# Twelve of sixteen token tiles loaded with columns as rows and normalized there by VectorE

## The chip, the cores and the metric

One Trainium2 chip, one core. The metric is the device time of one execution in microseconds. Engine names as the profile has them: PE is TensorE's matmul (PEld its weight load), DVE is VectorE, ACT is ScalarE, POOL is GpSimd, SP is SyncE, which issues most DMAs. A name with q (SPq, PEq) is the instruction queue of an engine.

## The reference, cut to what matters

```python
x = A_x                                   # 1 x 2048 x 576, float32
xn = layernorm(x)                         # per token: (x - mean) / sqrt(var + 1e-5)
qkv = xn @ wqkv                           # 576 x 1728; 32 heads of 18
phi = lambda t: where(t > 0, t + 1, exp(t)) + 1e-6
kv = einsum("bhsd,bhse->bhde", phi(k), v); z = sum over s of phi(k)
o = (phi(q) @ kv) / (phi(q) @ z + 1e-6)
s = o @ wo
g = silu((gelu(xn @ w_gate) * (xn @ w_up)) @ w_down)   # 576 -> 4608 -> 576
out = x + s * g
```

Every product contracts over the columns of `xn`, so the matmuls want `xn` with its 576 columns on the partitions and the tokens along the free dimension. In memory `x` has one token per row.

## The kernel before, in words

**Tiles.** The 2048 tokens are 16 tiles of 128 (P = 128); four tiles are a block of 512 (TT = 4, TBN = 512), so there are four blocks, `tb` 0 to 3. The 576 columns are two halves of 288 (`j` = 0, 1), each laid out as three chunks of 128 rows, the last 32 rows (KR) repeated to fill the third chunk. A float32 product is made from words: a rounded high word and a low word of each operand, so an operand tile `xo` has five slots (three high chunks, two low ones; the low word of the third chunk stands within it), in tiles named `xo_B`. `xf` holds the same half block in full float32; differences of `xf` tiles (`SUMS`: T1, T3, T2, T4) are operands for a later stage in which the gate and up products are made with fewer multiplications.

**One tile's way.** `load_x` brings a tile with tokens on the partitions. `spread` takes mean and variance on DVE (`bn_stats`, `bn_aggr`) and starts the root on ACT (Ln, Exp); `scales` ends it on DVE; `center` subtracts the mean and multiplies by the scale, one DVE operation of 768 columns with a mean and a scale per partition. `turn` makes six PE transposes (two halves of three chunks) into two PSUM tiles `xt`. `place` copies them on ACT into the high word of `xo` and subtracts on DVE for the low words (a `tensor_sub` of 256 columns on 128 partitions and one of 128 columns on 32, per half). `save` copies the PSUM tiles on ACT into `xf`.

**The stage of the tiles.** `kv_tile(t)` is one round. `x_mm(t, c)`, c = 0 to 2, multiplies tile t by the weights of k and v and of the last columns of q, 14 matmuls each into one PSUM bank. Between them stand `turn(t + 1)`, `place(t + 1)` and `save(t + 1)`; `k_post` (min on DVE into `e_k`, max on DVE into `pk`, Exp on ACT, add on POOL), `v_post` (ACT copies), `kv_mm(t - 1)`, which adds `pk` times `va` into two PSUM banks kept for the whole stage (`kv_a`, `kv_b`), and `q_parts` and `q_post` for the q columns (`w_q`; an add twice on POOL). The q columns of a tile are turned by PE too (`q_turn`), behind the six transposes of `turn`, into a free part of the same PSUM tiles, and copied by `q_keep` into `ph4`. `x_next` is `spread`, `scales` and `center` for the tile two ahead. Tiles 4 to 7 also prepare q's weights (`prep_q`: one ACT copy, three POOL subtractions). Between tiles 7 and 8 stand eight q products (`q_store`), after tile 15 eight more (`q_hold`). `form` builds T1 to T4 of the first two blocks and `keep` stores them in device memory, with SP's DMA queue; `difference` makes the sums.

**Order.** All engines' orders are written out by hand: every operation goes through `pin`, which keeps its engine's program order, and each engine takes its instructions in that order. Waits between engines come from the tiles that the operations share. Tiles of a pool take turns in their buffers: PSUM has six banks of the common kind (`bank`), `b0` to `b15` and `m0` to `m2` are single buffers (`big`, `mid`) that hold one tile after another, so a load into a buffer waits for the last reader of what was in it. The x tiles stand in b14 and b15 by pairs; `xf` of the first two blocks in m0, m1, m2 and b13, of the others in m0, m2, b13 and m1.

**After the tiles.** `den`, `scale`, `halve` and `s_mm` end the attention (up to about 290 us), then 36 gate and up products (`matrix`) and the down product (`down_all`) take the rest. The change touches none of these, but for the place of one helper tile.

The line numbers of the profile: L170 is the transposes of `turn`, L420 those of `q_turn`, L93 all other matmuls of this stage, L87 ACT's operations, L90 DVE's, L96 POOL's, L99 all DMAs.

## Time and profile before

| | |
|---|---|
| time, median of 3 runs (lowest to highest) | 1498.84 us (1497.77 to 1499.46) |
| the profiled execution's own time | 1497.99 us |
| its span, first to last instruction | 1496.3 us |
| PE, DVE, ACT, POOL busy | 1487.2, 1061.4, 561.6, 540.3 us |
| granted TensorE clock, mean over the span | 1.000 |
| transposes of x on PE (L170) | 96, from 8.0 us to 172.5 us |
| transposes of q on PE (L420), beside those of the last two tiles | 14, from 32.4 us to 172.6 us |

A row of the timeline has the start and the length in us, engine, line, operation, the tiles written and read, and how many in a row; in brackets the idle time of the engine before it and what ended it. A row of the groups has count, busy time, mean of one in ns, and idle time in front of them. A row of the waits has who waited for whom, the sum in us, how often, and the longest. Ends of matmuls are modelled, so the distance between two starts is what a PE operation costs.

### The profile page before, as it was taken

The numbers are of one execution on the slowest core, as the hardware profiler recorded it, in microseconds if no ns is written. First come the engines' busy times: TensorE is split into PE (matmuls) and PEld (weight loads), VectorE is DVE, ScalarE is ACT, GpSimd is POOL, SyncE is SP. The second block draws the span as 40 slices with busy tenths as digits, with TensorE's granted clock in tenths as the row PEclk, the third lists the DMA queues.
The fourth block names the chain that finished last, engine by engine and source line by source line (L and its number), as shares of the span: only waits on it lengthen the run. The fifth ranks groups of instructions, "written<-read, shape, count | busy, mean of one in ns | idle before, by whom it ended". The sixth has DMA issues, their size and how long they took to land.

```text
span 1496.3 us, 22479 instructions
## 1 busy us (share of the span) xinstructions
PE 1487.2 (99%) x8399; PEld 1333.1 (89%) x8399; DVE 1061.4 (71%) x1602; ACT 561.6 (38%) x1047; POOL 540.3 (36%) x521
## 2 busy tenths in 40 slices
PE   9999999999999999999999999999999999999998
PEld 8989989988888888888888888888899999999998
DVE  7576476377787877788877788787785466555765
ACT  5435345333222232232232332222445454445443
POOL 5442430145655544655544565554410020000120
PEclk9999999999999999999999999999999999999999
DMA  5423105543443333443423444433697766686873
GB/s 206 147 101 154 58 6 197 193 175 144 172 172 136 144 109 130 173 173 136 160 106 135 154 173 151 157 118 124 216 334 250 233 211 228 227 285 225 298 245 120
DMA packets 112215, 257.15 MB, mean 172 GB/s; under 512 B 10138, under 2 KB 38682, under 8 KB 110058
## 3 DMA queue, kind: packets, MB, share of 16 engines
q1 hardware_dynamic: 110330, 246.41, 46.0%
q0 software_dynamic: 1632, 8.91, 1.6%
q8 instruction: 66, 1.08, 0.3%
q10 hardware_dynamic: 144, 0.39, 0.1%
q14 instruction: 43, 0.35, 0.1%
HBM read 157.73 MB, written 97.91 MB: 171 GB/s over the span
## 4 chain that ended last, share of the span: by engine, by line
PE 97%; DVE 2%; issue 0%; ACT 0%; DMA 0%; POOL 0%; ACTq 0%; DVEq 0%; POOLq 0%
PE bd L971 27%; PE al L765 15%; PE de L765 15%; PE ga L765 15%; PE be L765 8%; PE kv L93 7%; PE s L93 4%; PE q L93 3%; PE kv_a L93 1%; PE xt L170 1%; PE d L93 0%; PE kw L93 0%; PE b L93 0%; DMA x<-in_xe_dram 0%; DVE wkv L90 0%
## 5 line engine op out<-in xcount | busy, mean ns | idle before, releaser
L971 PE MATMUL bd<-t,s 128*128 128x288 f32 x3024 | 401.2, 295 | 0.0
L971 PEld LDWEIGHTS bd<-t,s 128*128 128x128 f32 x3024 | 400.9, 188 | 0.3 <-DVE u L90 0.2
L90 DVE TENSOR_TENSOR s<-sr,s 128x512 fp32r<-128x512 f32 x252 | 176.1, 738 | 119.8 <-ACT s L87 116.0
L87 ACT ACTIVATE s<-sr 128x512 fp32r<-128x512 f32 x252 | 149.0, 626 | 188.9 <-PE bd L971 130.5
L96 POOL TENSOR_TENSOR hs<-h,h 128x512 f32<-128x512 f32 x68 | 94.7, 1402 | 202.5 <-DVE h L90 199.8
L87 ACT ACTIVATE h<-h 128x512 f32<-128x512 f32 x108 | 67.0, 633 | 244.7 <-POOL sm L96 124.1
L96 POOL TENSOR_TENSOR sx<-sx 128x288 f32<-128x288 f32 x24 | 27.9, 1181 | 322.9 <-DVE sx L90 321.8
L93 PE MATMUL kv<-wkv,xo_B 128*128 128x416 f32 (+1 forms) x672 | 130.8, 349 | 0.0
L93 PEld LDWEIGHTS kv<-wkv,xo_B 128*128 128x128 f32 x672 | 121.1, 188 | 1.2 <-POOL wkv L96 0.2
L90 DVE TENSOR_TENSOR wa<-raw,wa 128x256 fp32r<-128x256 f32 x72 | 81.1, 1127 | 51.1 <-ACT wa L87 50.0
L96 POOL TENSOR_TENSOR sm<-raw 128x384 f32<-128x384 f32 x72 | 76.0, 1055 | 109.2 <-DMA raw<-in_wgu_dram 83.5
L90 DVE TENSOR_TENSOR h<-h,u 128x512 f32<-128x512 f32 x108 | 95.7, 886 | 3.7
L87 ACT ACTIVATE wa<-sm 128x1152 fp32r<-128x1152 f32 x36 | 41.8, 1161 | 135.3 <-PE de L765 135.3
L96 POOL TENSOR_TENSOR td<-td 128x288 f32<-128x288 f32 x72 | 70.9, 985 | 51.2 <-DMA td<-in_wd_dram 47.0
L90 DVE TENSOR_TENSOR wa<-sm,wa 128x768 fp32r<-128x768 f32 x72 | 62.9, 873 | 36.9 <-ACT wa L87 36.0
L90 DVE TENSOR_TENSOR wb<-raw,wb 128x256 fp32r<-128x256 f32 (+1 forms) x108 | 73.0, 676 | 7.3 <-ACT wb L87 5.8
L90 DVE TENSOR_TENSOR wb<-sm,wb 128x256 fp32r<-128x256 f32 x72 | 60.9, 845 | 20.6 <-ACT wb L87 20.0
L87 ACT ACTIVATE u<-al 128x512 f32<-128x512 f32 x72 | 40.8, 592 | 88.4 <-PE al L765 88.4
L765 PE MATMUL al<-xo_B,wa 128*128 128x512 f32 x252 | 63.0, 389 | 0.0
L765 PE MATMUL al<-xr_B,wa 128*128 128x512 f32 x252 | 63.0, 389 | 0.0
L765 PE MATMUL be<-xo_T,wa 128*128 128x512 f32 x252 | 63.0, 389 | 0.0
L765 PE MATMUL be<-xr_T,wa 128*128 128x512 f32 x252 | 63.0, 389 | 0.0
(168 smaller groups left out, 2766.5 us busy)
## 6 DMA issues: line engine op xcount, KB each, us to landing
sr<-hs SPq DMA_DIRECT2D x252, 256.0 KB
hs<-h SPq DMA_DIRECT2D x68, 512.0 KB
raw<-in_wgu_dram SPq DMA_DIRECT2D x36, 768.0 KB
hs<-hs SPq DMA_DIRECT2D x102, 256.0 KB
td<-in_wd_dram SPq DMA_DIRECT2D x18, 576.0 KB
td<-td SPq DMA_DIRECT2D x18, 576.0 KB
tr<-td SPq DMA_DIRECT2D x16, 576.0 KB
tr<-in_wd_dram SPq DMA_DIRECT2D x12, 576.0 KB
```

Source lines behind the costliest of these rows:

```text
L87: pin(nc.scalar.activation(*args, **kw))
L90: pin(getattr(nc.vector, op)(*args, **kw))
L93: pin(nc.tensor.matmul(*args, **kw))
L96: pin(getattr(nc.gpsimd, op)(*args, **kw))
L170: pin(nc.tensor.transpose(xts[n][j][:, k, :], xs[:, j, k * P : (k + 1) * P], ident))
L765: nc.tensor.matmul(o, w[0:rows, wi, :], xop[0:rows, xi, :], start=(start and n == 0), stop=(n == len(PASSES) - 1), skip_group_check=True,)
L971: nc.tensor.matmul(banks[j][:, 0:HALF], hw[n, s][:, a, t * P : (t + 1) * P], w[:, c, g % 4], start=(new and g == 0 and m == 0), stop=(g == ...
```

## The change

Tiles 4 to 15 are also given to the kernel as `xt`, the raw x of blocks 1 to 3 with columns as rows, in the layout of `xf`; `load_turned` brings half a block by one DMA (128 x 1536 elements) straight into `xf`. Two tiles at a time, `spread` and `scales` work as before from rows of `x` (576 columns a token, without the repeated ones); then the means and scales of the 256 tokens (512 numbers) go by one DMA into device memory and come back by another onto all 128 partitions, behind the x tiles in their buffer (`mr`). `norm` subtracts and multiplies with them in `xf`: per half block part of two tiles one `tensor_sub` and one `tensor_mul` of 3 x 2 x 128 columns. `place` of these tiles reads `xf` instead of PSUM. `center`, `turn` and `save` are left for tiles 0 to 3 alone: 24 transposes of x instead of 96, each other operation of the product unchanged.

With that move: `q_turn` takes two tiles at once into a bank of its own behind `x_mm(t, 1)` of even tiles, and copies 256 columns; the min in `k_post` goes from DVE to ACT (as Relu of the negative); `place(t + 1)` stands ahead of `x_mm(t, 0)`; `form` also starts the load of a later half block into the buffer it has just read; the differences of the last two blocks stand behind tiles 13 and 15; `load_x(1)` goes from ACT's queue to SP's, ahead of the first weights; `w_q` and a helper tile (`one`) have other buffers.

```diff
@@ -118,18 +119,36 @@
     def load_x(n, k, eng=None):
 
         if n % 2 == 0:
-            xstat[n // 2] = big(14 + n // 2 % 2, [P, 2, 2, 3 * P], F32, f"x_{n}")
-        dma(
-            out=xstat[n // 2][:, n % 2 : n % 2 + k],
-            in_=xe[n * P : (n + k) * P].rearrange("(t p) j d -> p t j d", p=P), eng=eng,
-        )
+            xstat[n // 2] = big(14 + n // 2 % 2, [P, 2 * D + 2 * P2], F32, f"x_{n}")
+        if n < TT:
+            o = x_of(n)[:, None] if k == 1 else xstat[n // 2][:, 0 : 12 * P].rearrange(
+                "p (t j d) -> p t j d", t=2, j=2)
+            dma(out=o, in_=xe[n * P : (n + k) * P].rearrange("(t p) j d -> p t j d", p=P), eng=eng)
+        else:
+            dma(
+                out=xstat[n // 2][:, 0 : 2 * D].rearrange("p (t d) -> p t d", t=2),
+                in_=x[n * P : (n + 2) * P].rearrange("(t p) d -> p t d", p=P),
+            )
+
+    def x_of(n):
+
+        w = 6 * P if n < TT else D
+        return xstat[n // 2][:, n % 2 * w : (n % 2 + 1) * w].rearrange("p (j d) -> p j d", j=2)
+
+    def load_turned(tb, j):
+
+        s, b = divmod(tb, 2)
+        nm = BS[b][j]
+        at_ = XM[s][nm]
+        xf[s][nm] = (mid if at_ < 3 else big)(at_, [P, 3, TBN], F32, f"xf_{s}_{nm}")
+        dma(out=xf[s][nm], in_=xt_d[j, :, :, (tb - 1) * TBN : tb * TBN])
 
     def spread(n0, n):
 
         bn = sb.tile([P, TT, 12], F32, tag="bn", bufs=2, name=f"bn_{n0}")
         mv = sb.tile([P, 2 * TT, 2], F32, tag="mv", bufs=4, name=f"mv_{n0}")
         for t in range(n):
-            xs = xstat[(n0 + t) // 2][:, (n0 + t) % 2]
+            xs = x_of(n0 + t)
             for j in range(2):
                 vec("bn_stats", out=bn[:, t, 6 * j : 6 * j + 6], in_=xs[:, j, 0:HALF])
             vec("bn_aggr", out=mv[:, t, :], in_=bn[:, t, :])
...
@@ -142,6 +161,7 @@
     def scales(n0):
 
         n, mv, st = mom.pop(n0)
+        far = n0 >= TT
...
@@ -150,28 +170,42 @@
         else:
             vec("scalar_tensor_tensor", c, r, -0.5, r, op0=ALU.mult, op1=ALU.mult)
             vec("tensor_mul", c, c, v)
-            vec("scalar_tensor_tensor", c, c, 1.5, r, op0=ALU.add, op1=ALU.mult)
+            o = mv[:, 0:n, 1] if far else c
+            vec("scalar_tensor_tensor", o, c, 1.5, r, op0=ALU.add, op1=ALU.mult)
+        if far:
+
+            d = dr.tile([2, 2, P], F32, name=f"mr_{n0}")
+            dma(out=d.rearrange("t q p -> p (t q)"), in_=mv[:, 0:2, :].rearrange("p t q -> p (t q)"))
+            mr = xstat[n0 // 2][:, 2 * D :]
+            dma(out=mr, in_=d.rearrange("t q p -> (t q p)").partition_broadcast(P))
+            return
         for t in range(n):
             scale_of[n0 + t] = mv[:, t, 0:1], c[:, t : t + 1]
 
...
-    def turn(n, new=bank, q=True):
-
-        xs = xstat[n // 2][:, n % 2]
+    def norm(n, js=(0, 1)):
+
+        tb, t = divmod(n, TT)
+        s, b = divmod(tb, 2)
+        mr = xstat[n // 2][:, 2 * D :].rearrange("p (t q c) -> p t q c", t=2, q=2)
+        for j in js:
+            f = xf[s][BS[b][j]][:, :, t * P : t * P + P2].rearrange("p k (t c) -> p k t c", t=2)
+            for q, op in enumerate(("tensor_sub", "tensor_mul")):
+                vec(op, f, f, mr[:, None, :, q, :].to_broadcast([P, 3, 2, P]))
+
+    def turn(n, new=bank):
+
+        xs = x_of(n)
         tiles = [new(f"xt_{n}_{j}") for j in range(2)]
         xts[n] = [t[:, 0 : 3 * P].rearrange("p (k t) -> p k t", k=3) for t in tiles]
         for j in range(2):
             for k in range(3):
                 pin(nc.tensor.transpose(xts[n][j][:, k, :], xs[:, j, k * P : (k + 1) * P], ident))
...
@@ -182,14 +216,13 @@
             nm = BS[b][j]
             if t == 0 and 0 in words:
                 xo[s][nm] = big(2 * b + j, [P, 5, TBN], F32R, f"xo_{s}_{nm}")
-            o, v = xo[s][nm], xts[n][j]
+            o, v = xo[s][nm], xts[n][j] if n < TT else xf[s][nm][:, :, c]
...
@@ -370,11 +403,11 @@
         o, e, src = pks[t], es[t], pkv[t, c]
         cs = slice(0, TW) if c == 0 else slice(TW, D)
         src = src[:, 0 : cs.stop - cs.start]
-        vec("tensor_scalar", e[:, cs], src, 0.0, None, op0=ALU.min)
+        act(e[:, cs], src, AF.Relu, scale=-1.0)
         vec("tensor_scalar", o[:, cs], src, 0.0, EPS, op0=ALU.max, op1=ALU.add)
         if c == 1:
             es.pop(t)
-            act(e, e, AF.Exp)
+            act(e, e, AF.Exp, scale=-1.0)
             pool("tensor_add", o, o, e)
...
-    def q_turn(ts, banks):
-
-        for t, (b, i) in zip(ts, banks):
-            o = b[:, i * P : (i + 1) * P]
-            pin(nc.tensor.transpose(o, pqt.pop(t)[:, 0:2], ident))
-            pqx[t] = o
-
-    def q_keep():
-        for t in sorted(pqx):
-            tb, i = divmod(t, TT)
-            if i == 0:
-                ph4[tb] = gl_tile([P, TBN], f"ph4_{tb}")
...
+    def q_turn(t):
+
+        tb, i = divmod(t, TT)
+        b = bank(f"qx_{t}")
+        for n in range(2):
+            pin(nc.tensor.transpose(b[:, n * P : (n + 1) * P], pqt.pop(t + n)[:, 0:2], ident))
+        if i == 0:
+            ph4[tb] = gl_tile([P, TBN], f"ph4_{tb}")
+            if tb < 2:
+                ph_d[tb] = dr.tile([P, NHG, TBN], F32, name=f"phd_{tb}")
+        act(ph4[tb][:, i * P : (i + 2) * P], b[:, 0:P2], AF.Copy)
+        if i == 2 and tb < 2:
+            dma(out=ph_d[tb][:, 4, :], in_=ph4[tb])
...
-    def kv_tile(t, mid_=(), end=(), after=()):
-
-        ahead = t % (2 * TT) != 2 * TT - 1
+    def kv_tile(t, early=(), end=(), after=()):
+
+        if t % (2 * TT) != 2 * TT - 1 and t > TT - 1:
+            place(t + 1)
         x_mm(t, 0)
-        if ahead:
-            turn(t + 1)
         k_post(t, 0)
+        run(list(early))
         x_mm(t, 1)
-        if ahead:
+        if t % 2 == 0 and t % (2 * TT):
+            q_turn(t - 2)
+        if t == TT - 1:
             place(t + 1)
-            save(t + 1)
-        run(list(mid_))
         k_post(t, 1)
...
@@ -597,7 +627,7 @@
         buf = big(15, [P, n + TBN], F32R, "aux")
         at["sel"] = sel = buf[:, 0:n].rearrange("p (g j) -> p g j", g=NHG)
         at["rd"] = rd = buf[:, n : n + TBN]
-        at["one"] = one = tmp([H, NHG, P], "self")
+        one = at["one"]
...
@@ -1089,8 +1119,8 @@
 
     turn_idle(22)
     load_x(0, 1)
+    load_x(1, 1)
     load_kv(0, 0)
-    load_x(1, 1, nc.scalar)
     load_kv(0, 1)
...
@@ -1134,6 +1164,8 @@
     x_mm(0, 0, of((1, LO), (1, MIX)))
     x_mm(1, 0, of((1, LO), (1, MIX)))
     load_x(4, 2)
+    for j in range(2):
+        load_turned(1, j)
...
     def x_next(n):
 
-        if n % 2 == 0:
-            spread(n, 2)
-            scales(n)
-        center(n)
-
+        spread(n, 2)
+        scales(n)
+
+    def form(nm, tb, j):
+
+        o = build(0, nm, 12)
+        load_turned(tb, j)
+        keep(0, nm, o)
 
     x_mm(2, 0)
-    turn(3, q=False)
+    turn(3)
     kv_mm(0)
-    q_turn((0,), [(xtb.pop(3)[0], 3)])
     k_post(2, 0)
+    x_next(4)
     x_mm(2, 1)
+    q_turn(0)
     place(3)
     save(3)
     load_x(6, 2)
@@ -1187,25 +1223,33 @@
     v_post(2, 1)
     x_mm(2, 2)
     kv_mm(1)
-    x_next(4)
     v_post(2, 2)
     q_parts(2)
     q_post(2)
...
     for n in range(3, 2 * TT):
-        ends = []
-        if n < 2 * TT - 2:
-            ends.append(lambda n=n: x_next(n + 2))
+        early, ends, after = [], [], []
+        if n == 3:
+            early.append(lambda: norm(4))
+        if n == 3:
+            after.append(lambda: x_next(6))
+        if n == 4:
+            after.append(lambda: norm(6))
         if n >= TT:
             j, c = divmod(n - TT, 2)
             prep_q(c, j)
             if n == TT + 1:
                 load_q(1)
-        if n == 2 * TT - 1:
-            ends += [lambda i=i: difference(0, i) for i in range(3)]
-        kv_tile(n, end=ends)
-        if n in (4, 6):
-            load_x(n + 4, 2)
+        if n == 5:
+            after.append(lambda: x_next(8))
+        if n == 6:
+            after += [lambda i=i: difference(0, i) for i in range(2)]
+        if n == 7:
+            ends.append(lambda: difference(0, 2))
+            after.append(lambda: form("T1", 2, 0))
+        kv_tile(n, early, ends, after)
+        if n in (4, 5):
+            load_x(2 * n, 2)
         if n == TT:
...
     behind = {
         0: [lambda: kv_mm(N0 - 1), lambda: difference(0, 3)],
-        1: [lambda: spread(N0, 2), lambda: scales(N0)],
-        2: [lambda: center(N0), lambda: form("T1")],
-        3: [lambda: spread(N0 + 2, 2), lambda: scales(N0 + 2)],
-        4: [lambda: turn(N0), lambda: place(N0)],
-        5: [lambda: center(N0 + 1), lambda: form("T3")],
-        6: [lambda: save(N0)],
+        1: [lambda: q_turn(N0 - 2)],
+        2: [lambda: form("T3", 2, 1), lambda: norm(N0, (0,))],
+        3: [],
+        4: [lambda: norm(N0, (1,)), lambda: load_x(N0 + 4, 2)],
+        5: [lambda: place(N0)],
+        6: [lambda: x_next(N0 + 2)],
         7: [],
     }
     for i in range(8):
         q_store(*divmod(i, 4))
         run(behind[i])
...
     for n in range(N0, 2 * N0):
-        ends = []
-        if n < 2 * N0 - 2:
-            ends.append(lambda n=n: center(n + 2) if n == N0 else x_next(n + 2))
-        after = [lambda n=n: form("T2" if n == N0 else "T4")] if n in (N0, N0 + 2) else []
+        early, ends, after = [], [], []
+        if n % 2 == 0 and n < 2 * N0 - 2:
+            after.append(lambda n=n: norm(n + 2))
+        if n in (N0, N0 + 1):
+            form_ = ("T2", 3, 0) if n == N0 else ("T4", 3, 1)
+            after.append(lambda f=form_: form(*f))
+        if n in (N0 + 1, N0 + 3):
+            after.insert(0, lambda n=n: x_next(n + 3))
+        if n == N0:
+            after.insert(1, lambda: load_x(N0 + 6, 2))
         if n == 2 * N0 - 3:
             ends.append(load_wo)
+            after.append(lambda: difference(1, 0))
         if n == 2 * N0 - 2:
             after.append(make_sel)
         if n == 2 * N0 - 1:
-            after.append(copy_sel)
-            ends += [lambda i=i: difference(1, i) for i in range(3)]
-        kv_tile(n, end=ends, after=after)
-        if n in (N0, N0 + 2):
-            load_x(n + 4, 2)
-    def last_turn():
-        b = bank("q_last")
-        q_turn(sorted(pqt), [(b, 0), (b, 1)])
-        q_keep()
+            after += [copy_sel, lambda: difference(1, 1), lambda: difference(1, 2)]
+        kv_tile(n, early, ends, after)
 
     q_hold(2, 7, [
-        [lambda: kv_mm(2 * N0 - 1), kv_done, last_turn, lambda: difference(1, 3)],
+        [lambda: kv_mm(2 * N0 - 1), kv_done, lambda: q_turn(2 * N0 - 2), lambda: difference(1, 3)],
         [lambda: kv_wo(4)],
...
@@ -1341,6 +1382,8 @@
     xs = A_x.reshape(S, D)
     xh = xs.reshape(S, 2, HALF)
     xe = np.concatenate([xh] + 3 * [xh[:, :, 2 * P :]], axis=2)
+    xt = xe[TBN:].reshape(S - TBN, 2, 3, P).transpose(1, 3, 2, 0)
+    xe = xe[:TBN]
```

More of the change, by code (lines that the diff above doesn't have):

```diff
@@ L170, in turn @@
                 pin(nc.tensor.transpose(xts[n][j][:, k, :], xs[:, j, k * P : (k + 1) * P], ident))
-        if q:
-            q_turn([t for t in sorted(pqt) if t < n - 1], [(t, 3) for t in tiles])
-        else:
-            xtb[n] = tiles
     def place(n, js=(0, 1), words=(0, 1)):
@@ L348, in block_kernel @@
     left = {}
-    pkv, pks, vas, es, pqt, pqx, ph4, ph, ph_d = ({} for _ in range(9))
+    pkv, pks, vas, es, pqt, ph4, ph, ph_d = ({} for _ in range(8))
     def x_mm(t, c, passes=None, new=bank):
@@ L401, in q_parts @@
     def q_parts(t):
-        w = tmp([P, 4, Q4], f"w_q{t}")
-        src, o, e = pkv[t, 2][:, CW[2] - Q4 : CW[2]], w[:, 2], w[:, 3]
+        w = sb.tile([P, 3, Q4], F32, tag="wq", bufs=3, name=f"w_q{t}")
+        src, o, e = pkv[t, 2][:, CW[2] - Q4 : CW[2]], w[:, 0], w[:, 2]
         vec("tensor_scalar", e, src, 0.0, None, op0=ALU.min)
@@ L411, in q_post @@
         w = pqt[t]
-        act(w[:, 3], w[:, 3], AF.Exp)
-        for i in range(2):
-            pool("tensor_add", w[:, i], w[:, 2], w[:, 3])
-    def q_turn(ts, banks):
-        for t, (b, i) in zip(ts, banks):
-            o = b[:, i * P : (i + 1) * P]
-            pin(nc.tensor.transpose(o, pqt.pop(t)[:, 0:2], ident))
-            pqx[t] = o
-    def q_keep():
-        for t in sorted(pqx):
-            tb, i = divmod(t, TT)
-            if i == 0:
-                ph4[tb] = gl_tile([P, TBN], f"ph4_{tb}")
-                if tb < 2:
-                    ph_d[tb] = dr.tile([P, NHG, TBN], F32, name=f"phd_{tb}")
-            act(ph4[tb][:, i * P : (i + 1) * P], pqx.pop(t), AF.Copy)
-            if i == TT - 1 and tb < 2:
-                dma(out=ph_d[tb][:, 4, :], in_=ph4[tb])
+        act(w[:, 2], w[:, 2], AF.Exp)
+        for i in (1, 0):
+            pool("tensor_add", w[:, i], w[:, 0], w[:, 2])
+    def q_turn(t):
[10 more added lines that the diff above has]
+            dma(out=ph_d[tb][:, 4, :], in_=ph4[tb])
     def run(todo, n=None):
```

17 lines of the change are left out of this document (8 added, 9 removed).

## The prediction

> **What bounds the kernel now.** I read the page first: how busy each engine is, and the chain of work that ended last.
>
> ```profile
> PE 1487.2 (99%) x8399; PEld 1333.1 (89%) x8399; DVE 1061.4 (71%) x1602; ACT 561.6 (38%) x1047; POOL 540.3 (36%) x521
> PE 97%; DVE 2%; issue 0%; ACT 0%; DMA 0%; POOL 0%; ACTq 0%; DVEq 0%; POOLq 0%
> ```
>
> PE is busy for 1487.2 of 1496.3 us and 97% of the chain. So what PE need not do comes off the end, if the engines that feed it still deliver in time. The stage to read is the one from 20 to 190 us, where the 16 token tiles pass. This is PE's timeline there, around tiles 5, 6 and 7 (columns: start, length, operation, count, and in brackets what ended idle time).
>
> ```profile
> 61.19 5.34 PE L93 MATMUL kv<-wkv,xo_B 128*128 128x416 f32 x28
> ...
> 70.05 0.82 PE L170 MATMUL xt<-ident,x 128*128 128x128 f32 x6
> 70.71 0.27 PE L420 MATMUL xt<-ident,w_q 128*128 128x128 f32 x1
> 70.74 5.34 PE L93 MATMUL kv<-wkv,xo_B 128*128 128x416 f32 x28
> ...
> 76.89 7.96 PE L93 MATMUL kv<-wkv,xo_B 128*128 128x416 f32 x42
> 84.69 1.05 PE L93 MATMUL kv_a<-pk,va 128*127 128x126 f32 x8
> ...
> 85.67 1.41 PE L93 MATMUL q<-xo_B,wq 128*128 128x512 f32 x5
> ```
>
> No row has a bracket: PE runs without a gap. From 61.19 to 70.74 is one tile with its six turns of x and one turn of q, 9.55 us. Tile 7 turns nothing and takes 76.89 to 85.67, 8.78 us. Where PE does wait in this part is in the view of waits up to 230 us:
>
> ```profile
> PE xt L170 <- DVE x L90: 1.6, 2, 1.3
> PE xt L420 <- POOL w_q L96: 0.4, 1, 0.4
> PE q_last L420 <- POOL w_q L96: 0.3, 1, 0.3
> ```
>
> **What goes from PE.** Seven turns make 9.55 - 8.78 = 0.77 us, so six make 0.66; the same comes out of the starts, 70.05 to 70.71. The change takes away `turn` of tiles 4 to 15: 12 x 0.66 = 7.9 us, none of it beside other PE work. The 16 turns of q stay, now in pairs behind `x_mm(t, 1)`: no change counted.
>
> **Waits that go.** Of the two waits of 1.6 us for DVE's x, the longest (1.3) is for the very first tile; the other 0.3 is `turn(2)`. In the new order the min of `e_k` has left DVE, so `center(2)` no longer queues behind it. The turn of q tile 0 (0.4) now stands one `x_mm` later. The last turn (0.3) waited because three differences stood ahead of `q_parts(15)` on DVE; now they stand behind it. Together 1.0 us. What is late next: nothing within 2 us, since each of these turns then has its operand before PE reaches it.
>
> **The start.** `load_x(1)` moves from ACT's queue to SP's, ahead of the first weights. The first tile no longer shares the DMA engines with it and lands earlier, the weights behind it land when they did, as the bytes ahead of them are the same. The gain lies between 0 and the 1.3 us above; I take 0, because PE's next matmuls need those weights, not x.
>
> **What DVE gets.** These are DVE's, POOL's and ACT's groups of the stage 113 to 187.5 us (the second eight tiles), one of POOL's from 38 to 77, and the busy time of the stage (PE, PEld, DVE, ACT, POOL).
>
> ```profile
> L90 DVE TENSOR_SCALAR x<-x,mv,st 128x768 f32<-128x768 f32 x6 | 4.1, 680 | 0.2
> L90 DVE TENSOR_SCALAR e_k<-kv 128x416 f32<-128x416 f32 x8 | 4.7, 593 | 12.6 <-PE kv L93 9.8 <-POOL w_q L96 2.7
> L90 DVE TENSOR_SCALAR e_k<-kv 128x160 f32<-128x160 f32 x8 | 2.6, 324 | 4.6 <-PE kv L93 4.5
> L90 DVE TENSOR_TENSOR xo_T<-xf_B,xo_T 128x1024 fp32r<-128x1024 f32 x3 | 4.0, 1348 | 3.8 <-ACT xo_T L87 3.8
> L90 DVE TENSOR_TENSOR xo_T<-xf_B,xo_T 32x512 fp32r<-32x512 f32 x3 | 2.0, 681 | 0.0
> L90 DVE TENSOR_TENSOR xo_B<-xt,xo_B 128x256 fp32r<-128x256 f32 x14 | 6.0, 425 | 0.9
> L90 DVE TENSOR_TENSOR xo_B<-xt,xo_B 32x128 fp32r<-32x128 f32 x14 | 4.0, 283 | 0.4
> L90 DVE BATCH_NORM_STATS2 bn<-x 128x6 f32<-128x288 f32 x8 | 3.2, 438 | 0.1
> L90 DVE BATCH_NORM_AGGREGATE mv<-bn 128x2 f32<-128x12 f32 x4 | 0.8, 209 | 0.1
> L90 DVE SCALAR_TENSOR_TENSOR st<-st 128x2 f32<-128x2 f32 x4 | 0.7, 162 | 0.9 <-ACT st L87 0.8
> L96 POOL TENSOR_TENSOR pk<-pk,e_k 128x576 f32<-128x576 f32 x8 | 12.4, 1546 | 40.9 <-ACT e_k L87 40.9
> L96 POOL TENSOR_TENSOR w_q<-w_q 128x64 f32<-128x64 f32 x14 | 4.2, 321 | 6.7 <-ACT w_q L87 6.7
> L96 POOL TENSOR_TENSOR wq<-rq,wq 128x256 fp32r<-128x256 f32 x3 | 2.2, 735 | 1.0 <-ACT wq L87 0.7
> L87 ACT ACTIVATE xo_B<-xt 128x384 fp32r<-128x384 f32 x14 | 6.1, 490 | 14.2 <-PE xt L420 14.2
> L87 ACT ACTIVATE st<-mv,eps_t 128x2 f32<-128x2 f32 x2 | 0.6, 296 | 2.3 <-DVE mv L90 2.3
> L87 ACT ACTIVATE st<-st 128x2 f32<-128x2 f32 x2 | 0.4, 203 | 0.1
> 113.00:187.50 74.50, 74.50 (x457) 73.81 (x456) 43.34 (x110) 33.52 (x100) 24.65 (x44) 1.00 0.29 107
> ```
>
> DVE is busy 43.34 of 74.5 us, so 5.55 us in a tile of 9.55. Of that `center` (0.68) and the two mins of `e_k` (0.59 + 0.32) go. What comes is `norm`: four tensor-tensors of 768 columns for two tiles. No row has 768; 512 take 0.68, 1024 take 1.35, so about 1.01 each, 2.0 us a tile. DVE then has 5.55 - 0.68 - 0.91 + 2.0 = 6.0 us in a tile of PE that is now about 8.78 + 0.11 = 8.9: two thirds. ACT loses two saves as long as its 0.49 us copy and takes the mins, 416 and 160 columns, for about 0.53 + 0.30: no more than before, 33.52 of 74.5 us. So on the averages neither becomes the bound, and DVE's new work is covered by PE's. What decides is whether one tile's chain is late.
>
> **The new wait.** Mean and scale go out by one DMA in 4-byte pieces and come back by another that waits for it; `norm` stands first in line on DVE and waits for the second. Queued behind it on DVE are `place` of the next tile and the `pk` of `k_post`, and PE waits for `place`. On SP, the load of the next pair, `load_q` and the stores of `ph4` queue behind the reading back; none is needed within a tile. Three rows bound a round trip: the first load, and the last stores at the end of the span.
>
> ```profile
> core 0 of [0], span 1496.3 us
> 0.81 0.39 SPq L99 DMA_DIRECT2D x<-in_xe_dram  x1
> 4.81 0.82 DVE L90 BATCH_NORM_STATS2 bn<-x 128x6 f32<-128x288 f32 x2 [4.81 <-DMA x<-in_xe_dram]
> 1493.11 0.89 SPq L99 DMA_DIRECT2D out_dram<-sx  x2
> ```
>
> From issue to use is 4.0 us for the first load, among others; the last store is issued by 1494.0 and the span ends 2.3 us later. Two in a row: 4.6 to 8.0 us. Mine are small, but in 512 pieces: I take 6, nearer the short one.
>
> How long may it take? The statistics of a pair cost 4 x 0.44 + 2 x 0.21 on DVE, 0.30 + 0.20 on ACT and four small DVE operations of 0.16: about 3.3 us. For pairs 6, 10, 12 and 14 they run behind tile n and `norm` behind tile n + 1, a PE tile later: 8.9 - 3.3 = 5.6 us before DVE stands still. After that `norm` (4.0) and `place` (2 x (0.43 + 0.28) = 1.4) must be done in the 8.9 us of the next tile: 3.5 us to spare. PE is late only from 9.1 us on. Pair 4 has its statistics behind `x_mm(2, 0)` and its `norm` behind `x_mm(3, 0)`: a tile, a `turn` and one `kv_mm` (84.69 to 85.67, 1.0 us) apart, 8.9 + 0.66 + 1.0 - 3.3 = 7.3; behind it only two thirds of a tile are left, some 6 us for the 5.4: about 7.9. Pair 8 has the whole q stage. At 6 us all fit with 2 us or more, at 8.0 only just.
>
> That room is shared with POOL. Here are DVE and POOL when tile 7 ends, where DVE runs tensor-tensors with both inputs in SBUF:
>
> ```profile
> 83.02 6.43 DVE L90 TENSOR_TENSOR xf_B<-xf_B,xf_B 128x1536 f32<-128x1536 f32 x3
> 90.83 1.75 DVE L90 TENSOR_TENSOR xf_B<-xf_B,xf_B 128x1536 f32<-128x1536 f32 x1
> ...
> 83.67 2.37 POOL L96 TENSOR_TENSOR pk<-pk,e_k 128x576 f32<-128x576 f32 x1 [3.33 <-ACT e_k L87]
> ```
>
> One costs 1.75; three cost 6.43 instead of 5.25, and POOL's add takes 2.37 where its mean is 1.55: each waited for the other. `norm`, and `place` of tiles 4 to 15, which now reads `xf` in SBUF where it read PSUM (0.43 us with no such spread), become operations of this kind. POOL brings 1.55 + 2 x 0.32 = 2.2 us into a tile, and 3 x 0.735 more in tiles 4 to 7 where it prepares q's weights. At most that much is lost in a tile: 2.2 of a room of some 2.5, 4.4 in tiles 4 and 6. Tiles 8 and 9 also have a `form` (1.35 + 0.68) on DVE between `norm` or the statistics and `place`: 0.4 + 4.0 + 2.0 + 1.4 + 2.2 = 10.0 against 8.8. So PE should lose between 0 and 2 x 1.9 (tiles 4 and 6) plus 2 x 1.2 (8 and 9), 6.2 us if every operation meets one of POOL's; I take 1.5, a quarter, as DVE has a third of the time free.
>
> The Trainium skill (SBUF — State Buffer, "Who interferes with whom") says of this that a DVE instruction with two SBUF inputs and a GpSimd instruction that reads SBUF exclude each other for the whole instruction, whoever starts first; the rows above agree (6.43 for three of 1.75). By that rule the `place` of the change is exposed and that of before was not, which speaks against the change; at its worst it gives the rival of that name below, 1498.5 instead of 1491.4.
>
> **Sum.** -7.9 - 1.0 + 1.5 = -7.4 us. The profiled execution took 1497.99 (span 1496.3 and 1.7 around it): 1490.6. The median of the runs before is 1498.84: **1491.4 us**.
>
> **The rivals.**
> - *Nothing new waits.* All of POOL's work falls beside DVE's free time. 1498.84 - 8.9 = 1489.9, and up to 0.9 less from the start. For it: the round trip fits with room. Against: tiles 8 and 9.
> - *DVE becomes the bound through POOL (the shared port).* By the same numbers with nothing overlapping, a tile costs DVE 6.0 + 2.2 = 8.2, under 8.9; tiles 4 to 7 cost 10.4, 1.5 over each; tiles 8 and 9 10.2, 1.3 over. 4 x 1.5 + 2 x 1.3 = 8.6 lost, 1498.5: no difference. Against: it needs every operation to meet.
> - *Slower: the reading back.* If the scattered 4-byte store is slow, PE stands for every microsecond over about 9, in five pairs. It decides from 9 + 8.9 / 5 = 10.8 us; at 13 us PE loses 20, 1510. Against: both rows above stay under 8.0 for two. For: no row shows a DMA in 512 pieces of 4 bytes.
> - *The turns were covered.* If PE had to wait there anyway (for a bank, for `pk`), taking them away gives waits instead and only the 1.0 us, 1497.8. Against: no bracket in PE's rows, and tile 7 without turns runs at the same pace.
>
> By the Trainium skill (DMA: Bandwidth & Descriptors, "Specifications") a piece under 512 B costs a read-modify-write in the DMA engine; no trace here shows what that takes for 4 bytes.
>
> **How the numbers follow.** Forecast 0.55, nothing new waits 0.30, DVE bound 0.05, slower by the reading back 0.06, covered 0.04. 0.2% is 3.0 us, about what a measurement of this kernel can tell from no change. Faster 0.55 + 0.30 = 0.85, same 0.05 + 0.04 = 0.09, slower 0.06. The range goes from 1489.0 (all gains and 0.9 from the start) to 1495.0 (8.9 less some 5 of the 6.2 us that POOL could cost); it leaves out 0.15 of the chance.
>
> **What would show it.** Right: PE's tiles 8.9 us apart with 24 turns of x in all; no PE wait for DVE over 1 us in this stage; DVE's wait for the DMA before `norm` at or under 1 us for pairs 6 to 14; the rest of the program the same, earlier by 7 us. Wrong: brackets on `kv` rows of PE that name DVE xo_B or ACT xo_B; norm rows far over 1.0 us; a DMA wait ahead of `norm` of several us, the same in each pair.

## The result, and the profile after

The changed kernel takes 1532.72 us (median of 5 runs, 1531.51 to 1534.58) against 1498.84 for the kernel before: ratio 1.0229, 95% interval 1.0215 to 1.0244. It is 33.9 us slower where 7.4 less were forecast. The profiled execution took 1531.51, span 1529.8.

The page of the changed kernel, busy time and chain:

```profile
PE 1492.1 (98%) x8327; PEld 1333.9 (87%) x8327; DVE 1064.7 (70%) x1582; ACT 561.4 (37%) x1047; POOL 548.1 (36%) x521
PE 87%; DMA 5%; DVE 2%; ACT 1%; issue 1%; POOL 0%; SPq 0%; POOLq 0%; ACTq 0%; DVEq 0%
```

PE does 72 matmuls less and yet is busy for 4.9 us more, and a chain that was 97% PE now has 5% DMA. Both numbers matter: some of the time is waiting, some is work that became slower. The view of waits from 25 to 235 us, rows of PE, DVE and SP (waited for: us in total, times, longest):

```profile
PE kv L93 <- ACT xo_B L87: 25.2, 5, 6.5
PE kv L93 <- DVE xo_B L90: 2.1, 2, 1.8
PE qx L454 <- POOL w_q L96: 1.0, 1, 1.0
DVE xf_B L90 <- DMA x<-mr: 35.3, 4, 10.7
SPq L99 <- DMA mr<-mv: 47.4, 6, 8.3
```

The first two rows are what the prediction named as signs that it is wrong: PE waits for `place`, which waits for `norm`, which waits for the reading back. The chain of waits around pair 6 shows how long that is:

```profile
61.91 0.17 DVE mv L90
62.08 0.02 issue
62.10 8.17 DMA mr<-mv
70.27 0.02 issue
70.28 6.45 DMA x<-mr
76.73 0.02 issue
76.76 0.97 DVE xf_B L90
```

A store of 2 KB takes 8.17 us from issue to landing, the reading back 6.45: 14.6. Over the six pairs the round trip took 12.1 to 14.6. The DMA engines are not busy for that long. These are all packets from 62.1 to 63.4 us, and from there to 70.2:

```profile
DMA packets 528, 0.00 MB, mean 2 GB/s; under 512 B 528, under 2 KB 528, under 8 KB 528
DMA packets 2, 0.02 MB, mean 4 GB/s; under 512 B 0, under 2 KB 0, under 8 KB 0
```

The 512 pieces, among the 528 small packets, are through 1.3 us after the issue, and the landing comes 6.9 us later; what happens in between no view shows. PE's timeline at tiles 4 to 6:

```profile
48.48 0.29 PE L93 MATMUL kv_b<-pk,va 128*73 128x72 f32 x2
54.42 7.53 PE L93 MATMUL kv<-wkv,xo_B 128*128 128x416 f32 x28 [5.66 <-ACT xo_B L87]
65.44 7.96 PE L93 MATMUL kv<-wkv,xo_B 128*128 128x416 f32 x42
74.12 0.29 PE L93 MATMUL kv_b<-pk,va 128*73 128x72 f32 x2
79.32 3.05 PE L93 MATMUL kv<-wkv,xo_B 128*128 128x416 f32 x7 [4.90 <-ACT xo_B L87]
```

The gaps are one half of it. The other is that the 28 matmuls behind a gap take 7.53 us, where the same 28 took 5.34 before. The clock fell to a half five times, each time for 6.83 us; these are the five stretches (us; busy time of PE, PEld, DVE, ACT, POOL; granted clock, DMA share, GB/s):

```profile
51.66:58.49 6.83, 4.07 (x11) 3.48 (x12) 5.40 (x9) 2.83 (x9) 0.89 (x1) 0.50 0.38 152
78.97:85.80 6.83, 6.48 (x18) 5.80 (x19) 5.58 (x15) 3.26 (x11) 2.11 (x4) 0.50 0.99 415
147.24:154.06 6.82, 4.98 (x13) 4.25 (x14) 5.61 (x13) 2.86 (x10) 1.24 (x1) 0.50 0.53 136
164.30:171.13 6.83, 3.54 (x9) 2.88 (x10) 4.04 (x8) 3.86 (x7) 0.00 (x0) 0.50 0.24 47
198.44:205.26 6.82, 4.47 (x12) 3.87 (x13) 5.69 (x10) 3.18 (x10) 0.80 (x1) 0.50 0.41 132
```

PE works 23.5 us of these at half pace, so it does 11.8 us of work less than it would. The Trainium skill (TensorE: Matmul & The Clock Gate, "HAM oscillation — how this bites in real kernels") warns of just this: a gap in PE's work of more than about 3.4 us throttles the clock to a half, and the work behind the gap starts cold. The rows of this kernel agree, in the halving and in what follows the gaps, which are of 3.5 us and more; the prediction left it out. Shorter gaps in the experiments do not fit (last section).

**Where the 41 us between forecast and result are**, in the profiled execution: gaps ahead of tiles 4, 6, 10 and 14, 5.7 + 4.9 + 5.3 + 4.6 = 20.5; a gap of 6.8 ahead of tile 11, which experiment 1 explains; 1.0 at a turn of q; 11.8 of half clock; 1.9 at the start, where PE's run of 59 matmuls begins at 14.79 and not at 12.84. That is 42.0; less the 1.5 forecast for POOL, which was not paid, 40.5. The spans differ by 1529.8 - (1496.3 - 7.4) = 40.9. This is PE's account; it does not say what each part would give back if it alone went (experiment 4).

### The profile page after: what moved, and what is told of

Same layout as the page of the kernel before. It is cut to its first block, busy times and chain, and to the rows that moved or that the text cites. A ratio compares the mean times of both kernels' runs of the same rounds, so it can differ in the third digit from the quotient of the medians.

```text
span 1529.8 us, 22292 instructions
## 1 busy us (share of the span) xinstructions
PE 1492.1 (98%) x8327; PEld 1333.9 (87%) x8327; DVE 1064.7 (70%) x1582; ACT 561.4 (37%) x1047; POOL 548.1 (36%) x521
## 4 chain that ended last, share of the span: by engine, by line
PE 87%; DMA 5%; DVE 2%; ACT 1%; issue 1%; POOL 0%; SPq 0%; POOLq 0%; ACTq 0%; DVEq 0%
PE bd L1001 26%; PE al L795 15%; PE ga L795 15%; PE de L795 15%; PE be L795 7%; PE s L93 3%; PE kv L93 2%; PE q L93 2%; DMA mr<-mv 2%; DMA kept_T<-xo_T 2%; DMA x<-mr 1%; DVE xf_B L90 1%; DMA xf_B<-in_xt_dram 1%; PE d L93 0%; PE kw L93 0%
## 5 line engine op out<-in xcount | busy, mean ns | idle before, releaser
L93 PE MATMUL kv<-wkv,xo_B 128*128 128x416 f32 (+1 forms) x672 | 141.6, 369 | 29.8 <-ACT xo_B L87 26.6
L93 PEld LDWEIGHTS kv<-wkv,xo_B 128*128 128x128 f32 x672 | 129.8, 201 | 35.5 <-ACT xo_B L87 27.6
L90 DVE TENSOR_TENSOR wb<-sm,wb 128x256 fp32r<-128x256 f32 x72 | 60.8, 845 | 20.5 <-ACT wb L87 20.0
L90 DVE TENSOR_TENSOR u<-u,ga 128x512 f32<-128x512 f32 x72 | 49.3, 686 | 20.0 <-PE ga L795 19.3
```

The source lines that it names most:

```text
L90: pin(getattr(nc.vector, op)(*args, **kw))
L93: pin(nc.tensor.matmul(*args, **kw))
```

## Experiments

The theory: the round trip is the cause, and the half clock follows from its gaps. The rival: DVE, with `norm` and `place` on two SBUF inputs, is late beside POOL, which the prediction priced at 1.5 us and at 6.2 at most. Each kernel ran beside the kernel before on the same chip; ratios are to it.

**1. No round trip.** `load_x` fills the columns that `norm` reads, and the two DMAs of `scales` go:

```diff
+            dma(out=xstat[n // 2][:, 2 * D :], in_=x[n * P : (n + 1) * P, 0 : 2 * P2])
-            dma(out=d.rearrange("t q p -> p (t q)"), in_=mv[:, 0:2, :].rearrange("p t q -> p (t q)"))
-            dma(out=mr, in_=d.rearrange("t q p -> (t q p)").partition_broadcast(P))
```

> The changed kernel, but the values that norm subtracts and multiplies by do not make the round trip: they are filled in by one plain load of 256 KB from x, long before (the part left out is mean and scale of tiles 4 to 15; norm computes with other numbers, with the same instructions). Theory (the round trip of 11 to 15 us makes PE late five times, and each gap is followed by 6.8 us of half clock): the five gaps and the half clock go, 28 + 12 us of 1532.7, so 1490 to 1494, granted clock 1.00. Rival (DVE with its new two-input operations is late beside POOL): most of the gaps stay, since norm and place cost the same, and the time stays above 1510. If both, in between, with waits of PE for DVE xo_B left.

1498.26 us (1.0002, 0.9992 to 1.0011): 34.5 us are gone, but the time is 4 above what the theory allowed. All of PE's waits from 25 to 235 us, and the chain to the one gap that is left, ahead of tile 11:

```profile
PE kv L93 <- ACT xo_B L87: 3.6, 1, 3.6
PE kv L93 <- DVE xo_B L90: 0.2, 1, 0.2
128.47 0.55 SPq L99
...
129.08 10.01 DMA kept_T<-xo_T
...
139.11 1.49 ACT xo_T L87
...
140.62 1.23 DVE xo_T L90
```

The rival falls: `norm` and `place` cost DVE no less than in the changed kernel (`norm` 1.00 us, 0.96 there), and PE waits for `place` only ahead of tile 11, where a second cause appears. `form` builds T1, T3, T2 and T4 in one buffer (12). The change moved T4's `form` from behind tile 10 to behind tile 9, one tile behind T2's, and put `load_turned`, 768 KB, ahead of T2's store. The store took 10.0 us (5.5 for that of 126.32 us in the kernel before), ACT waited to write T4 into the buffer, and `place(11)` stood behind that on DVE. In the changed kernel the same store took 14.4 us and the gap is 6.8. There a store of 4-byte pieces is issued while it runs, as in experiment 4, where it took 14.2; in experiments 1, 2, 3, 5, 9, 10 and 11, which have none there, it took 9.8 to 10.4. So some of that gap too may come from the round trip; no run separates it.

**2. Mean and scale spread by PE.** Four transposes of a broadcast column for each pair, into a bank that `norm` reads, 24 in all:

```diff
+                pin(nc.tensor.transpose(
+                    far_mr[n][:, t, q, :], mv[:, t, q : q + 1].to_broadcast([P, P]), ident))
```

> The changed kernel, but mean and scale come onto all partitions through PE: four transposes of a column broadcast along the free axis for each pair of tiles, into a PSUM bank from which norm reads. No DMA is in the way. 24 more transposes of 0.11 us: +2.6 us of PE. Theory (round trip): 1492 to 1496, no gap over 1 us ahead of tiles 4, 6, 10, 12, 14, granted clock 1.00. Rival (DVE late beside POOL): norm now has one input in PSUM, so this would gain more than the kernel without round trip and come out below it, rather than 2.6 us above it.

1498.12 us (0.9994, 0.9984 to 1.0003), 2 us above the theory and as much as without a round trip: the 2.6 us of transposes are offset by a smaller gap ahead of tile 11, 2.1 + 1.0 us with 3.4 us of half clock. The rival had it below experiment 1, and it is not: `norm` takes 0.95 us with one input in PSUM, hardly less than with both in SBUF.

**3. The same 2 KB in 128 pieces of 16 bytes**, so that a partition's four numbers stay together:

```diff
-            d = dr.tile([2, 2, P], F32, name=f"mr_{n0}")
-            dma(out=d.rearrange("t q p -> p (t q)"), in_=mv[:, 0:2, :].rearrange("p t q -> p (t q)"))
+            d = dr.tile([P, 2, 2], F32, name=f"mr_{n0}")
+            dma(out=d, in_=mv[:, 0:2, :])
```

> The changed kernel, but the same 2 KB of mean and scale are stored in 128 pieces of 16 bytes instead of 512 of 4, and norm reads them back with a stride of four columns. If the number of pieces sets the 8.2 us from issue to landing of the store, it becomes about 3 to 4 us and the time falls by some 20 us, with the half clock after the gaps, to about 1505 to 1515. If it is that the pieces are small, whatever their number, the store still takes about 8 us and the time stays at 1533 plus or minus 3. norm with a stride could cost DVE more than 0.96 us a piece of work; if so it is slower.

1513.69 us (1.0094, 1.0079 to 1.0109), inside the first case. SP's wait for the store, and the group of `norm` in this kernel and in the changed one (36 to 215 us):

```profile
SPq L99 <- DMA mr<-mv: 9.8, 6, 3.9
L90 DVE TENSOR_TENSOR xf_B<-xf_B,x 128x768 f32<-128x768 f32 x24 | 39.5, 1662 | 4.3 <-DMA x<-mr 3.6 <-DMA xf_B<-in_xt_dram 0.2
```

```profile
L90 DVE TENSOR_TENSOR xf_B<-xf_B,x 128x768 f32<-128x768 f32 x24 | 22.7, 958 | 37.6 <-DMA x<-mr 35.3 <-DMA xf_B<-in_xt_dram 1.8
```

Six stores are now waited for 9.8 us together instead of 47.4; four of them land 1.4 us after issue, the other two 2.2 and 4.3. A new price is that `norm`, reading with a stride of four columns, takes 1.66 us instead of 0.96, 2.8 us more for a pair. The gap ahead of tile 11 stands as in experiment 1 (4.2 us, with 6.8 of half clock). How the rest divides no run shows.

**4. PE kept busy in the gaps** by transposes that nobody reads:

```diff
+    IDLE = {4: 48, 6: 42, 10: 30, 12: 55, 14: 40}
+                pin(nc.tensor.transpose(b[:, 0:P], ident, ident))
```

> The changed kernel with transposes of the identity on PE, which nobody reads, ahead of the first matmul of tiles 4, 6, 10, 12 and 14 (48, 42, 30, 55, 40 of 0.11 us, so about as long as the gaps). The round trip stays. Theory (each gap of PE lets the clock fall to a half for 6.8 us, which costs about 2.4 us or more a time): the clock stays at 1.00, and the time falls by 10 to 13 us, to about 1520 to 1523. Rival (the half clock has another cause, or costs nothing on the way to the end): 1533, or more by what the transposes overrun the gaps.

1537.32 us (1.0261, 1.0246 to 1.0276): a miss for the theory, and what the rival had, 1533 or more by what the transposes overrun. One reason is plain: the gap that the 55 transposes were for stands ahead of tile 11, not 12, and they cost 6 us there. The other is instructive. The clock did stay at 1.00 around tiles 4, 6 and 14, and fell only twice, at 151.0 and 168.1, at the gaps ahead of tiles 10 and 11. At full pace the 28 matmuls of tile 4 are done 0.6 us sooner although they start later; the first matmuls of tiles 4 and 6:

```profile
54.94 1.03 PE L93 MATMUL kv<-wkv,xo_B 128*128 128x416 f32 x4 [0.93 <-ACT xo_B L87]
56.58 4.78 PE L93 MATMUL kv<-wkv,xo_B 128*128 128x416 f32 x24 [0.62 <-DVE xo_B L90]
80.14 1.02 PE L93 MATMUL kv<-wkv,xo_B 128*128 128x416 f32 x4 [1.73 <-ACT xo_B L87]
```

But tile 6 still begins at 80.14, where it began at 79.32 in the changed kernel: what sets it is the chain of statistics, store and reading back, which hangs on DVE and SP and not on PE's pace. Tile 7 begins at 90.06 instead of 91.44, so 1.4 us were won where some 5 of half clock went. So of the 11.8 us a part would have been waiting otherwise; how much was not settled for the later gaps.

**5. T4 in a buffer of its own**, on the kernel of experiment 2:

```diff
-        o = build(0, nm, 12)
+        o = build(0, nm, 3 if nm == "T4" else 12)
```

> The kernel with mean and scale spread by PE (1498.1), with one more edit: T4 is built in buffer 3, which is free then, instead of buffer 12, where T2 is until its store has landed. In the kernel with the PE spread, ACT's copy of T4 waited for T2's store (10.4 us from issue to landing), place(11) stood behind it on DVE, PE lost 2.1 + 1.0 us ahead of tile 11, and the clock stood at a half for 3.4 us after it. Theory (the two forms, one tile apart, meet in one buffer): both gaps and the half clock go, 4.5 to 5.5 us, so 1492.5 to 1494. Rival (DVE is late there by itself, with norm, two tensor-tensors of 1024 columns and place beside POOL): a gap of over 1 us stays ahead of tile 11, and 1496 or more.

1493.70 us (0.9967, 0.9955 to 0.9978), as the theory has it. All that PE waits for from 25 to 235 us, and PE's tiles 10 and 11:

```profile
PE s L93 <- DVE pq L90: 0.3, 1, 0.3
129.20 5.50 PE L93 MATMUL kv<-wkv,xo_B 128*128 128x416 f32 x28
138.64 7.96 PE L93 MATMUL kv<-wkv,xo_B 128*128 128x416 f32 x42
```

With both causes away the prediction's sum holds: 1498.84 - 8.9 + 24 x 0.11 + 2.0 at the start (tile 1 begins at 20.80, in the kernel before at 18.80) = 1494.6, and 1493.7 was measured, with nothing to pay for POOL (`place` has both inputs in SBUF here, `norm` one in PSUM).

**6. The statistics a tile earlier**, round trip as in the change, T4 in buffer 3:

```diff
+    x_next(4)
     x_mm(2, 0)
...
     load_q(0)
+    x_next(6)
```

and likewise `x_next(10)`, `x_next(12)` and `x_next(14)`.

> The changed kernel with its round trip as it is, 512 pieces of 4 bytes, but the statistics of pairs 4, 6, 10, 12 and 14, and with them the two DMAs, stand about a PE tile earlier in the order; T4 is built in buffer 3. Theory (the length of the round trip is all that hurts, and it has 18 us of room in place of 9): no gap over 1 us ahead of tiles 4 to 15, the clock at 1.00, and 1490 to 1494. Rival (the 4-byte pieces and the reading back also delay other transfers on the same queue, the load of the turned columns and the stores): PE still loses several us ahead of tiles 6 or 12, and 1498 or more.

1514.55 us (1.0107, 1.0090 to 1.0123): half of the loss is back, T4's own buffer included, and the rival is right about the rest. DVE hardly waits for the reading back now (first row), but for x (second); SP's queue shows why (start, length):

```profile
DVE xf_B L90 <- DMA x<-mr: 0.6, 1, 0.6
DVE bn L90 <- DMA x<-in_x_dram: 12.3, 2, 9.1
34.05 0.39 SPq L99 DMA_DIRECT2D mr<-mv  x1
42.54 0.34 SPq L99 DMA_DIRECT2D x<-mr  x1
42.98 2.10 SPq L99 DMA_DIRECT2D x<-in_x_dram  x1
```

The reading back waits on SP for the store's landing, 8.5 us, and the load of x for pair 6 stands behind it. DVE stands 9.1 us for that load at pair 6's statistics, ahead of `norm(4)`, and PE has a gap of 7.9 us ahead of tile 4. The gap ahead of tile 12, 4.9 us, has to do with T4's new buffer. `place(12)` writes its second half into buffer 3, and T4's store out of it took 17.0 us here, with a store of 4-byte pieces issued while it ran:

```profile
151.12 16.95 DMA kept_T<-xo_T
168.18 0.53 ACT xo_B L87
```

In experiment 5 the same store took 8.5 us, and nothing waited for it.

**7. The same, and x's tile 1 on ACT's queue again.**

```diff
     load_x(0, 1)
-    load_x(1, 1)
     load_kv(0, 0)
+    load_x(1, 1, nc.scalar)
```

> The kernel with the statistics a tile earlier and T4 in buffer 3, and the load of x's tile 1 back on ACT's queue, behind the first weights, as before the change. If that move of the change cost the 0.2 to 2.0 us by which PE's run of 59 matmuls starts later than before (12.84 there; 13.4 to 15.2 in the five kernels with the move), this one starts that run at 12.7 to 13.0 and is 1 to 2 us faster than the kernel with the earlier statistics: 1489 to 1492. If the start only varies from run to run, there is no difference between the two.

1511.08 us (1.0088, 1.0073 to 1.0103), 3.5 us under experiment 6; the 1489 to 1492 on record took that experiment's theory for granted. In the trace the start is 2.3 us sooner: tile 1 begins at 18.86 and not at 21.15. The profiled execution is the slowest of the four, though, only 1.0 us under that of experiment 6: the half clock behind the gap ahead of tile 4 lasts 10.2 us here and 6.8 there. PE's run of 59 matmuls here:

```profile
12.89 11.22 PE L93 MATMUL kv<-wkv,xo_B 128*128 128x416 f32 x59
```

In the kernel before it begins at 12.84.

**8. Small stores that nobody waits for**, one for each pair, on the kernel of experiment 2:

```diff
+                dma(out=dr.tile([4, P], F32, name=f"pr_{n0}").rearrange("i p -> p i"), in_=src)
...
+                d = dr.tile([4, P, 128], F32, name=f"pr_{n0}")
+                dma(out=d[:, :, 0].rearrange("i p -> p i"), in_=src)
```

> The kernel with mean and scale spread by PE, and one small store beside it for each pair of tiles that nobody waits for; only their time from issue to landing is of interest. Pairs 4 and 14: 512 pieces of 4 bytes, neighbours in memory side by side, as in the change. Pair 6: 128 pieces of 4 bytes. Pair 8: 256 pieces. Pair 10: 128 pieces of 4 bytes, 512 bytes apart in memory. Pair 12: 512 pieces, 512 bytes apart. If the number of pieces sets the time: about 8.2, 1.4 to 2, 4, 2, 8.2 us. If the pieces' size does: about 8 for all. If it is that neighbours share a line of memory: 8, 2 to 8, 4 to 8, and below 2 for pairs 10 and 12.

From issue to the landing of the last piece, by the trace's semaphore events, one reading each, among whatever other transfers ran:

| pieces | place in memory | us |
|---|---|---|
| 512 of 4 B (pairs 4, 14) | side by side | 9.45, 9.88 |
| 256 of 4 B | side by side | 8.87 |
| 128 of 4 B | side by side | 8.35 |
| 512 of 4 B | 512 B apart | 4.04 |
| 128 of 4 B | 512 B apart | 1.72 |

Neither the count nor the size by itself: a quarter of the pieces takes nearly as long, and the same pieces apart take less than a half or a fifth. The third case comes nearest, but had the 512 pieces apart below 2. What is slow is 4-byte pieces that lie side by side; how the memory handles them no run shows. The Trainium skill (DMA: Bandwidth & Descriptors, "Specifications") has a read-modify-write for pieces under 512 B. That alone does not tell the rows apart: 128 pieces of 4 B apart, or of 16 B side by side (experiment 3), are as small by that measure and land in 1.4 to 1.7 us at their fastest. The kernel took 1502.74 us in one run, 4.6 more than that of experiment 2.

**9. Spread by PE, T4 in buffer 3, x's tile 1 on ACT's queue** (the edits of 2, 5 and 7).

> The kernel with the spread by PE and T4 in its own buffer (1493.7), with the load of x's tile 1 back on ACT's queue behind the first weights. Theory (the move of that load costs 1.5 to 2.3 us at the start, as the first tiles of the kernels with and without it show): 1491.5 to 1492.5. Rival (the start varies by itself): 1493.7 again.

1491.84 us (0.9955, 0.9943 to 0.9968): 1.9 under experiment 5, as the theory has it, though the two intervals overlap, and the fastest of all versions.

**10. A short round trip**: DVE turns the columns into rows, four stores of 4 pieces of 128 B, the reading back as in the change; T4 in buffer 3.

```diff
+            vec("transpose", row, mv.rearrange("p t q -> p (t q)"))
+            for k in range(4):
+                dma(out=d.rearrange("t q p -> (t q) p")[:, 32 * k : 32 * k + 32], in_=row[32 * k : 32 * k + 4, :])
```

> The changed kernel with a round trip that is short: DVE turns the mean and scale of a pair by 32 by 32 blocks, so that they go to memory in 16 pieces of 128 bytes (four small stores) instead of 512 of 4, and come back as before, contiguous, so that norm runs at its 0.96 us; T4 is built in buffer 3. The round trip should take 2 to 2.5 plus 3.3 to 6 us, so 6 to 8, what the prediction took (6, up to 8). Theory (the prediction's room of 8 to 9 us was right and only the length of the round trip wrong): gaps of PE ahead of tiles 4, 6, 10, 12, 14 under 1 us, and 1491 to 1495. Rival (the room was overestimated too): gaps of 1 to 3 us in several pairs with half clock after them, 1498 to 1508.

1500.00 us (1.0008, 0.9999 to 1.0018), within the rival's times, with smaller gaps than it had. From the first store's issue to the reading back's landing it takes 5.8 to 7.1 us, 8.5 for pair 12, which is about what the prediction had assumed. The start costs 2.8 us in the profiled execution (PE's run of 59 begins at 15.63). PE's waits from 25 to 235 us:

```profile
PE kv L93 <- DVE xo_B L90: 2.8, 4, 1.3
PE qx L461 <- POOL w_q L96: 2.3, 1, 2.3
PE kv L93 <- ACT xo_B L87: 0.6, 1, 0.6
PE kv_a L93 <- POOL va L96: 0.5, 1, 0.5
```

None of the gaps is ahead of tiles 4 and 6: there the room was enough. In the second half 0.3 to 1.9 us are lost at tiles 8, 10, 11 and 12. Of the 1.9 ahead of tile 12 a part is not the round trip's: DVE also waits 0.6 us for the turned columns, and the third row is `place(12)` waiting for T4's store out of buffer 3. Ahead of `norm(14)` DVE stands 2.9 us for the reading back; it is so late with `pk` and `w_q` of tile 13 that POOL sets three tiles of the next stage to zero first (2.2 us), and a turn of q waits 2.3 us for POOL, with 3.4 us of half clock behind it. So at 6 to 8 us the round trip was not free either.

**11. The short round trip and ACT's queue.**

> The kernel with the short round trip, and the load of x's tile 1 back on ACT's queue. Where the short round trip is hidden: 1.5 to 2 us under that kernel, 1489 to 1493, the fastest of all as no transpose is added. Where it is not hidden: 1496 to 1506, still 1 to 2 us under it.

1498.49 us (0.9996, 0.9987 to 1.0004), 1.5 under experiment 10 and in the second of the two ranges: the round trip is not hidden. The run of 59 begins at 12.85.

**12. The kernel before with x's tile 1 on SP**, ahead of the first weights.

> The kernel before with only the one side change: x's tile 1 is loaded on SP's queue ahead of the first weights, as the change has it. Theory (the first weights land 1.6 us later because 0.4 MB stand ahead of them): 1500.0 to 1501.0, PE's run of 59 matmuls starts 1.2 to 2.3 us after 12.84. Rival, the prediction's step (x lands earlier, the weights land when they did): 1497.5 to 1499.0.

1500.24 us (1.0010, 1.0001 to 1.0019), 1.3 us more than before by the medians; the interval barely excludes no effect, but the trace shows the place, PE's run of 59 as before and as edited:

```profile
12.84 11.22 PE L93 MATMUL kv<-wkv,xo_B 128*128 128x416 f32 x59
```

```profile
10.13 0.64 PE L93 MATMUL kv<-wkv,xo_B 128*128 128x416 f32 x2 [1.91 <-ACT xo_B L87]
15.16 11.21 PE L93 MATMUL kv<-wkv,xo_B 128*128 128x416 f32 x59
```

What that run waits for is the weights. ACT's first copy of them, as before and as edited:

```profile
6.45 1.24 ACT L87 ACTIVATE wkv<-rw 128x1248 fp32r<-128x1248 f32 x1
```

```profile
8.46 1.24 ACT L87 ACTIVATE wkv<-rw 128x1248 fp32r<-128x1248 f32 x1 [2.95 <-DMA rw<-in_wkv_dram]
```

In the kernels with the load on SP the run begins at 13.4 to 15.6, with it on ACT at 12.8 to 12.9, and at 14.3 in experiment 9. Part of that spread is not the load's: in the profiled executions of experiments 1, 6, 8, 9 and 10 the clock stood at a half for 3.4 us somewhere between 8 and 15 us.

## Why the prediction was wrong, by its own steps

- **What goes from PE, 7.9 us: right.** Tiles without a stop stand 8.8 to 9.0 us apart (experiment 5: 58.44, 67.21, 76.20).
- **Waits that go, 1.0: right.** Without the two causes PE waits 0.3 us from 25 to 235 us.
- **The start, 0 to 1.3 of gain, taken as 0: wrong in sign.** It costs 1.3 to 2.3 us (experiment 12). The first tile does land earlier, as the step had it (DVE begins on it at 3.8 us and not 4.8), but the weights land later: ACT begins on them at 8.1 in the changed kernel and not at 6.5. The step weighed the bytes ahead of the weights and saw no change; x's tile 1 had gone by another queue, beside the weights, and now goes before them.
- **What DVE gets: right for `norm`**, estimated at 1.01 us and measured at 0.96. `place` was taken over at 1.4 us a tile and takes 2 x (0.52 + 0.36) = 1.8; in experiment 5 PE waits for neither.
- **POOL, 1.5 (0 to 6.2): nothing.** `place`'s 0.43 became 0.52, which may be the two meeting or the input that is now in SBUF. It stays in DVE's free time: in experiment 1, where `norm` too has both inputs in SBUF, PE waits at tile 11 alone, and in experiment 5 nowhere in the tiles.
- **The new wait, a round trip of 6 us (4.6 to 8.0): the step that failed.** It takes 12.1 to 14.6: 8.2 to 8.7 for the store and 3.3 to 6.5 for the reading back, each of which was taken at 2.3 to 4.0. Its bounds were two rows of large, contiguous transfers; the text itself noted that no row shows 512 pieces of 4 bytes, and took 6, nearer the short end, all the same. The rival "slower: the reading back" had the mechanism and its threshold, 10.8 us, and got 0.06.
- **That rival's size.** By its own rule, 4.7 us over 9 in five pairs, some 24, a time of about 1514. Three things came on top: the half clock behind each gap, the meeting of T2 and T4 in buffer 12 (priced as DVE time of `form` alone, not as a store that a later write waits for), and the start. The first is the largest, though experiment 4 shows that the half clock and the waiting partly cover each other.
- **The room, 9.1 us, and 7.9 for pair 4: about right.** In the changed kernel the round trip less the gap behind it is 8.7, 9.7, 7.7 and 9.7 us for pairs 4, 6, 10 and 14. In experiment 10 it is less in the second half: a round trip of 6.1 lost 0.8 us ahead of tile 10, where T2's `form` stands on DVE between `norm` and `place`, and one of 8.5 lost 1.9 ahead of tile 12, partly to other transfers.
- **What queues behind the new wait on SP** was named ("the load of the next pair") and priced at nothing. At 8.5 us a store that is not harmless: experiment 6.

## What to carry to other kernels

A DMA of a kind that the trace does not show has no upper bound from transfers of another kind: when its length decides the sign, say so in the chances, or lay the data out so that it resembles one that the trace does show. Few bytes are no sign of a short transfer. And a gap of PE costs more than its length, because of the half clock behind it, until something other than PE sets the next start. When two uses of a buffer are moved closer together, look at the store between them, and at what was put ahead of that store on its queue.

## What the runs showed of the hardware

- 4-byte pieces side by side in memory, from issue to landing: 8.2 to 8.7 us for 512 of them in the changed kernel, 8.4 to 12.6 in experiments 6 and 7, 9.5 and 9.9 in experiment 8, where 256 took 8.9 and 128 took 8.4. Apart, 4.0 for 512 and 1.7 for 128. 128 pieces of 16 B side by side, 1.4 in four of six.
- The reading back, 2 KB to every partition, took 3.1 to 6.9 us in all the kernels that do it; 256 KB of `phd` are stored in 2.0 at their fastest.
- In the changed kernel the half clock began 2.3 to 4.6 us after PE's work stopped, and lasted 6.8 us behind gaps of 3.5 us and more; behind one of 7.7 in experiment 7 it lasted 10.2. Gaps of 2.1 to 2.5 us (experiments 2, 3 and 10) were already followed by 3.4 us of it, and in experiment 11 so were three of 0.5 to 1.1 us that lay within 4.2 us; two of 2.2 and 2.6 us in experiment 3 were followed by none. By the Trainium skill (TensorE: Matmul & The Clock Gate, the section named above) it would take more than about 3.4.
- A tensor-tensor of 768 columns takes 0.96 us, and 1.66 when one input is read with a stride of 16 bytes.
